# A model of GpSimd's time in a kernel's placement planner, and zero multiplications where the output bank can't take them

## The chip, the cores and the metric

The kernel runs on one core of a Trainium2 chip. The core has five engines that run side by side, each through its own list of instructions in order: TensorE (PE) multiplies matrices into PSUM banks, VectorE (DVE) does elementwise work, ScalarE (ACT) does activations such as exp, GpSimd (POOL) does elementwise work on SBUF data, and SyncE (SP) issues DMAs. They meet through semaphores. The metric is the device time of one execution in microseconds (us); less is better.

## The reference

Two blocks of layers, run twice with the same weights, on x of 2048 rows and 512 columns. Weights and x are bfloat16.

```python
x = x + attention(layernorm(x), wqkv, wo)   # 32 heads of 16, softmax over all 2048 keys
x = x + ffn(layernorm(x), w1, w2)           # 512 -> 1792, silu, 1792 -> 512
x = x + attention(layernorm(x), wqkv, wo)
x = x + ffn(layernorm(x), w1, w2)

def layernorm(x): return (x - mean(x)) / sqrt(var(x) + 1e-5)
def attention(x, wqkv, wo):
    q, k, v = split_heads(x @ wqkv)
    p = softmax(q @ k.T * 16 ** -0.5)       # each of 32 heads: 2048 x 2048
    return join_heads(p @ v) @ wo
```

The 32 x 2048 x 2048 exponentials of each attention are most of the elementwise work.

## The kernel before

**The stream.** Attention of both layers is one stream of 1,024 steps after a first one. A step takes one tile of 128 keys for one group of heads and 512 queries: four heads, so four blocks of 128 x 512 scores. From the twelfth step on, ScalarE takes the exponentials of three blocks (one of 512 columns from its own bank, and a pair of 1,024 columns from one of two double banks; `exp`, L1140), and the fourth block, called d, is done without ScalarE: VectorE turns its scores into the bits of a 16-bit float (`d_y`, in `emit_d`, L1058), and GpSimd adds two constants to those bits for two further terms (`d_z`, in `other_terms`, L1078). In the first twelve steps ScalarE takes four blocks and the fourth shares the bank of d. Scores are multiplications with 32 rows (`score`, L909; tiles `s_ps` and `d_ps`); probabilities times v run every second step into one bank, `o_ps` (`to_o`, L933), which VectorE copies out at the end of a run of steps (`end_run`, L1038: `oA`, `oB`, `oC`, `oT`).

**The background.** Everything else (layer norms, the projections to q, k and v, the output projection, the feed-forward part) is cut into small parts and placed between the steps' instructions. These multiplications all write to one PSUM bank of their own, taken by `bank()`. They are generators that yield a `part(...)`, with what it costs TensorE or VectorE, ahead of each piece.

**The planner.** Engines take no decisions at run time. While the program is built, a `Model` keeps a time for TensorE (`pe`), ScalarE (`act`), VectorE (`dve`) and SyncE (`sp`), and after each step the loop hands out background parts as long as `fits` says that they end before ScalarE needs the next scores. A part may name something that it needs; `Background.done` holds the model's time at which that is ready. If a step gets no work for TensorE, `fill(3)` adds three groups of multiplications with a tile of zeros to the open `o_ps` bank, which leave its sums as they are. It adds none (returns 0) while no run is open in that bank or one of its four parts is still empty or already complete.

**Layer norms.** `ln_stats` (L386) has VectorE take mean and variance of two row tiles (L392, L394), and GpSimd make the reciprocal deviation `rstd` of both: an addition (L396), then a power (L397). `ln_chunk` (L433) has VectorE apply them, `xn` (L402), for the four row tiles of a chunk of 512 rows, and SyncE transpose each by DMA (L308). xn has three buffers, so the fourth norm of a chunk waits until the first transpose has landed. The norms of a chunk are placed by the planner, which in the kernel before knows nothing of GpSimd's time.

**The ends.** The stream is preceded by a prologue of some 16 us and followed by a tail of some 41 us (the last feed-forward chunk), in which instructions are written in a fixed order.

Of the kernel before, what the change touches and what calls it, by code (L numbers as in the profile page):

```python
# [24 lines left out]
def part(dve=0.0, pe=0.0, held=False, sums=False, need=None):  # L25

    return Part(held, pe, dve, sums, need)

class Background:
# [44 lines left out]
    def advance(self, item):  # L74
        if self.model:
            self.model.charge(item[2])
        try:
# [4 lines left out]
            else:  # L82
                home = [q for q in (self.outs, self.side, self.queue) if item in q][0]
                home.remove(item)
                self.done[item[0]] = self.model.landed if self.model else 0.0

    def heads(self, now):
        return [
            self.outs[0] if self.outs else None,
            self.head(now),  # L90
            self.prime(self.side[0]) if self.side else None,
        ]
# [17 lines left out]
class Model:  # L110
# [11 lines left out]
    TRANSPOSE = 1.27  # L122
    TRANSPOSED = 1.7
    DMA = 0.64

    def __init__(self, slack, margin):
        self.slack, self.margin = slack, margin
        self.pe = self.act = self.dve = self.ready = self.free = 0.0
        self.s1 = self.sd = self.copied = self.sp = self.landed = 0.0
        self.s2 = [0.0, 0.0]  # L130
        self.mode = None
        self.early = False
        self.evacuated = 0.0
# [37 lines left out]
    def pv(self, groups):  # L171
        self.pe = max(self.pe, self.copied)
        self.to("V")
        self.pe += self.GROUP * groups
        self.summed = self.pe + self.TO_DVE

    def transpose(self):
        self.sp = max(self.sp, self.dve + 0.1) + self.TRANSPOSE
# [40 lines left out]
def kernel(  # L219
# [39 lines left out]
    FILL = 3  # L259
# [85 lines left out]
    bg = Background()  # L345
# [40 lines left out]
    def ln_stats(c, tiles):  # L386
        n = len(tiles)
        mv = small.tile([P, n, 2], FP32, name="mv", tag="mv", bufs=5)
        for k, i in enumerate(tiles):
            yield part(0.69)  # L390
            st = small.tile([P, 6], FP32, name="st", tag="st")
            nc.vector.bn_stats(st[:], x_sb[c][:, i, :])  # L392
            yield part(0.2)
            nc.vector.bn_aggr(mv[:, k, :], st[:])  # L394
        rstd = small.tile([P, n, 1], FP32, name="rstd", tag="rstd", bufs=5)
        nc.gpsimd.tensor_scalar_add(rstd[:], mv[:, :, 1:2], float(EPS))  # L396
        nc.gpsimd.tensor_tensor(out=rstd[:], in0=rstd[:], in1=half[:, 0:n, :], op=ALU.pow)  # L397
        return mv, rstd
# [20 lines left out]
    def ln_pair(c, i):  # L419

        stats[c, i] = yield from ln_stats(c, (i, i + 1))

    def ln_transpose(i, xns, dst, copy=nc.vector.tensor_copy):

# [8 lines left out]
    def ln_chunk(c, dst):  # L433

        for i in (0, 2):
            mv, rstd = stats.pop((c, i))
            for u in range(2):
                yield part(0.45, need=("xn", xn_count[0] - XN_BUFS))
                xn = ln_apply(c, i + u, mv[:, u, :], rstd[:, u, :])
                transpose(dst[:, i + u, :, :], xn[:])  # L440
                bg.done["xn", xn_count[0]] = bg.model.landed
                xn_count[0] += 1
# [104 lines left out]
    def d_blocks(c):  # L547

        return [(kt, kt % 4) for kt in range(4 * c, 4 * c + 4)]

    def scale_v(L, c):

        n = len(d_blocks(c))
        VB[L, c] = vbpool.tile([P, n * 2 * VBW + 16], FP16, name="VB", tag="VB", bufs=7)
        nc.gpsimd.memset(VB[L, c][:, n * 2 * VBW :], 0.0)
        for i, (kt, j) in enumerate(d_blocks(c)):
            va = VA[L, c][:, kt % 4, 0 : 17 * H].rearrange("p (g j e) -> p g j e", j=4, e=34)
            for k, (_, w) in enumerate(TERMS):
                nc.gpsimd.tensor_scalar(
                    out=VB[L, c][:, (2 * i + k) * VBW : (2 * i + k + 1) * VBW].rearrange(  # L560
                        "p (g e) -> p g e", e=34
                    ),
                    in0=va[:, :, j, :],
                    scalar1=w,
                    scalar2=0.0,
                    op0=ALU.mult,
                    op1=ALU.add,
                )
# [168 lines left out]
    def warm(n, ps=None):  # L737

        if ps is None:
            ps = bank("warm")  # L740
        for i in range(n):
            nc.tensor.matmul(ps, lhsT=ident[:], rhs=w_qkv[:, i % CT, 0:D], start=True, stop=True)  # L742
# [114 lines left out]
    for g in range(NG):  # L857
        mine = [r for r in runs if r[3] == g]
        n = 0
# [46 lines left out]
    def score(blk, out):  # L906
        L, qc, pi, g, par, kt, j = blk
        r = slice(32 * j, 32 * j + 32)
        nc.tensor.matmul(  # L909
            out,  # L910
            lhsT=KT[L, kt // 4][r, g, (kt % 4) * P : (kt % 4 + 1) * P],
            rhs=QT[g][r, par, :],
            start=True,
            stop=True,
        )
# [157 lines left out]
    def other_terms(t, pr):  # L1073

        n = len(pr["ds"])
        for k, (off, _) in enumerate(TERMS):
            z = dpool.tile([P, 2, 512], U16, name=f"d_z{k}", tag=f"z{k}")
            nc.gpsimd.tensor_scalar(  # L1078
                out=z[:, 0:n, :].rearrange("p a b -> p (a b)"),
                in0=pr["y"][:, 0:n, :].rearrange("p a b -> p (a b)"),  # L1080
                scalar1=float(off),
                scalar2=1.0,
                op0=ALU.add,
                op1=ALU.mult,
            )
            for i, d in enumerate(pr["ds"]):
                d["rhs"].append((t + 3 + k, k + 1, z[:, i, :].bitcast(FP16)))

# [14 lines left out]
    with tc.manual_schedule(  # L1103
# [62 lines left out]
        for t in range(1, len(steps)):  # L1166
            a_blks, d_blks = steps[t]
            for L, qc, pi, g, par, kt, j in a_blks + d_blks:
                bg.ensure(q_of[L, qc, pi, g, par])
                if qc == 0:  # L1170
                    bg.ensure(("k", L, kt // 4, g))
            L, qc, pi, g, par, kt, j = a_blks[0]
            if t == len(steps) - NKT:
                load_w1_tail()
            if kt == kts_of[L, qc, pi, g, par][0]:
                for Lq, c, gq, n in q_next.get((L, qc, pi, g, par), []):
                    bg.add(("q", Lq, c, gq, n), proj_q(Lq, c, gq), first=True)
            s2 = score_pair()[:]
            n1 = len(a_blks) - 2
            s1 = [  # L1180
                psum["s"].tile([P, 512], FP32, name="s1_ps", tag=tag, bufs=1)[:]
                for tag in ("s1", "sd")[0:n1]
            ]
            for i in range(2):
                score(a_blks[n1 + i], s2[:, i, :])
            for i in range(n1):
                score(a_blks[i], s1[i])
            if n1 == 1:
                for blk in d_blks:
                    emit_d(t, blk)  # L1190
            m.scores(len(a_blks), len(d_blks))
            while after:
                after.pop()()
                m.sums()
            if t in pv_steps:
                m.pv(emit_pv(t, pv_step(t)))
            if t < D_LEAD:
                p = p_pre[:, 3 * t + 1 : 3 * t + 4, :]
                parts = [p[:, 0:n1, :], p[:, n1 : n1 + 2, :]]
            elif n1 == 1:  # L1200
                p = ppool.tile([P, 3, 512], BF16, name="p_sb", tag="p")
                parts = [p[:, 0:1, :], p[:, 1:3, :]]
            else:
                parts = [
                    dpool.tile([P, 2, 512], U16, name="p_z", tag=f"z{k}")[:].bitcast(BF16)
                    for k in range(2)
                ]
            p_tiles[t] = [p[:, i, :] for p in parts for i in range(p.shape[1])]
            for i in range(n1):
                exp(p_tiles[t][i], s1[i])  # L1210
            exp(flat(parts[1]), flat(s2))
            m.exps(len(a_blks))
            if t <= 4:
                bg.ensure(("v", 0, 0, t - 1))
            if t == 5:
                early[0] = m.early = False
            busy = t in pv_steps
            late = L == 0 or qc == 0
            while True:
                for item in bg.heads(t):  # L1220
                    if bg.fits(item) and (late or not item[2].pe or item[2].sums or t not in pv_steps):
                        break
                else:
                    break
                busy = busy or item[2].pe > 0
                bg.advance(item)
            if n1 == 2 and d_blks:
                m.late_d()
                emit_d(t, d_blks[0])
            if not busy and m.fill_fits(FILL):  # L1230
                n = fill(FILL)
                if n:
                    m.pv(n)
        t = len(steps) + 1
        emit_pv(t, pv_step(t))
        after.pop()()
# [36 lines left out]
```

## Time and profile before

| | us |
|---|---|
| median of three runs | 1564.99 (1564.02 to 1565.08) |
| the profiled execution, its own time | 1566.2 |
| its span, first to last instruction | 1564.1 |
| ScalarE busy in it | 1514.3 (97%) |
| TensorE busy | 1467.9 (94%) |
| GpSimd busy | 1113.9 (71%) |
| VectorE busy | 1080.1 (69%) |

The mean TensorE clock in it was 0.991 of the full one. In the profile, a group of instructions stands in one row: line, engine, operation, tiles out and in, shapes and count; then busy us and the mean ns of one; then the idle time of its engine just ahead of it, and which instruction ended most of that. A waits view lists who waited for whom, with the sum, the number and the longest wait in us. A timeline lists instructions in order of time: start, length, engine and line, how many were merged into the row, and the idle time before it with what ended it. Multiplications are pipelined and their ends are modelled, so busy TensorE isn't TensorE at its peak.

### The profile page before, as it was taken

To read this page: it belongs to the slowest core of one execution; us is meant where nothing else is said; L and a number is where in the kernel's file an instruction comes from. 1 tells how busy PE (TensorE), PEld (TensorE's weight loads), DVE (VectorE), ACT (ScalarE), POOL (GpSimd) and SP (SyncE) were. 2 spreads that over 40 slices of the span, in tenths; PEclk is the share of its full clock that TensorE was granted. 3 is DMA by queue.
4 is the path that set the end of the run, shared out by engine and by line. 5 is a ranking of instruction groups with operands and counts; after the bars stand their busy time and mean duration, and the time that the engine had idled before them with its cause. 6 is when DMAs were issued, how large, how long until landed. Compare 5 with 4: busy or idle time off the path is not lost. (4 is left out here: it accounts for less than half of the span.)

```text
span 1564.1 us, 34241 instructions
## 1 busy us (share of the span) xinstructions
PE 1467.9 (94%) x13361; PEld 464.9 (30%) x13361; DVE 1080.1 (69%) x1733; ACT 1514.3 (97%) x2191; POOL 1113.9 (71%) x1172
## 2 busy tenths in 40 slices
PE   7999998899999999899998999998999899999998
PEld 3222332232322322222322333322332232222225
DVE  6877677667776777667776667676667666676645
ACT  6999999999999999999999999999999999999993
POOL 2888776677876778667876778776777677776760
PEclk9999999999999999999999999999999999999999
DMA  4110013101121112201021010121012101120110
GB/s 138 32 28 2 5 35 65 28 19 44 45 45 28 31 25 50 51 17 42 20 49 42 11 35 9 25 58 32 18 46 62 29 19 30 45 48 22 37 47 14
DMA packets 149442, 55.84 MB, mean 36 GB/s; under 512 B 127776, under 2 KB 148768, under 8 KB 149280
## 3 DMA queue, kind: packets, MB, share of 16 engines
q1 hardware_dynamic: 149280, 53.65, 14.1%
q8 instruction: 105, 1.72, 0.5%
q14 instruction: 57, 0.47, 0.1%
HBM read 28.57 MB, written 4.19 MB: 21 GB/s over the span
## 5 line engine op out<-in xcount | busy, mean ns | idle before, releaser
L1140 ACT ACTIVATE p_sb<-s_ps 128x512 bf16<-128x512 f32 x2026 | 1466.6, 1100 | 9.4 <-PE d_ps L909 5.1
L1058 DVE TENSOR_SCALAR d_y<-d_ps 128x512 uint16<-128x512 f32 x1012 | 697.4, 689 | 404.4 <-PE d_ps L909 362.5
L909 PE MATMUL s_ps<-QT,KT 32*128 32x512 bf16 x3084 | 631.0, 383 | 59.1 <-ACT p_sb L1140 44.9
L909 PE MATMUL d_ps<-QT,KT 32*128 32x512 bf16 x1012 | 390.5, 386 | 9.1 <-DVE d_y L1058 6.0
L909 PEld LDWEIGHTS <-KT 32*128 32x128 bf16 x4096 | 187.1, 91 | 647.9 <-issue 595.1
L933 PE MATMUL o_ps<-p_sb,VA 128*32 128x512 bf16 x3039 | 312.3, 389 | 8.2 <-DVE oB L1038 1.1
L933 PE MATMUL o_ps<-d_y,VA 128*32 128x512 f16 x1012 | 153.7, 380 | 0.0
L933 PEld LDWEIGHTS <-VA 128*32 128x32 bf16 x4096 | 86.7, 95 | 160.9 <-issue 123.0
L711 PE MATMUL f_ps<-w_sb,hT 128*128 128x512 bf16 x392 | 104.0, 382 | 0.0
L933 PEld LDWEIGHTS <-VB 128*32 128x32 f16 x2024 | 78.5, 98 | 55.6 <-issue 1.0
L933 PE MATMUL o_ps<-w_qkv,zero 128*32 128x512 bf16 x1344 | 93.8, 385 | 0.0
L649 ACT ACTIVATE t_sb<-h_ps 128x512 f32<-128x512 f32 x98 | 86.0, 878 | 0.0
L652 DVE SCALAR_TENSOR_TENSOR hT<-t_sb,h_ps 128x512 bf16<-128x512 f32 x98 | 67.3, 687 | 22.5 <-ACT t_sb L649 22.3
L603 DVE TENSOR_TENSOR attn<-ot,rec 128x256 bf16<-128x256 bf16 x45 | 49.3, 1095 | 1.5
L1038 DVE CAST oT<-o_ps 128x512 bf16<-128x512 f32 x64 | 43.6, 681 | 7.7 <-PE o_ps L933 7.7
L402 DVE TENSOR_SCALAR xn<-x,mv,rstd 128x512 bf16<-128x512 bf16 x64 | 42.0, 669 | 4.9 <-DMA fT<-xn 2.7
L392 DVE BATCH_NORM_STATS2 st<-x 128x6 f32<-128x512 bf16 x64 | 43.6, 680 | 2.1 <-DMA x<-in_A_x_dram 2.1
L711 PEld LDWEIGHTS <-hT 128*128 128x128 bf16 x392 | 29.2, 97 | 46.4 <-issue 25.0
L933 PEld LDWEIGHTS <-zero 128*32 128x32 bf16 x1344 | 25.6, 95 | 40.6 <-issue 28.5
L466 PE MATMUL q_ps<-xnT,w_qkv 128*128 128x512 bf16 x136 | 36.6, 389 | 0.0
L466 PE MATMUL k_ps<-xnT,w_qkv 128*128 128x512 bf16 x128 | 35.4, 390 | 0.9 <-DVE xnT L431 0.9
L396 POOL TENSOR_SCALAR rstd<-mv 128x2 f32<-128x2 f32 x32 | 7.7, 239 | 40.0 <-DVE mv L394 38.5
(2298 smaller groups left out, 2093.6 us busy)
## 6 DMA issues: line engine op xcount, KB each, us to landing
wo<-in_A_wo_dram SPq DMA_DIRECT2D x8, 512.0 KB, 3.8
QT<-q SPq DMA_DIRECT2D x240, 16.0 KB, 1.8
x<-in_A_x_dram SPq DMA_DIRECT2D x7, 512.0 KB, 4.2
out_dram<-x SPq DMA_DIRECT2D x16, 128.0 KB, 1.7
w_sb<-in_B_w_dram SPq DMA_DIRECT2D x1, 1792.0 KB, 13.9
w_qkv<-in_A_wqkv_dram SPq DMA_DIRECT2D x3, 512.0 KB, 7.4
w_tail<-in_B_w_dram SPq DMA_DIRECT2D x3, 512.0 KB, 6.9
ot<-oT SPq DMA_TRANSPOSE x45, 2.3
```

Source lines behind the costliest of these rows:

```text
L392: nc.vector.bn_stats(st[:], x_sb[c][:, i, :])
L402: nc.vector.tensor_scalar(out=xn[:], in0=x_sb[c][:, i, :], scalar1=mv[:, 0:1], scalar2=rstd, op0=ALU.subtract, op1=ALU.mult,)
L466: nc.tensor.matmul(ps.rearrange("p (t q) -> p t q", q=P) if len(r.shape) == 3 else ps, lhsT=lhs(ct), rhs=r, start=(ct == 0), stop=(ct == C ...
L603: nc.vector.tensor_tensor(out=attn[L, qc][:, :, P * g : P * (g + 1)].rearrange("p t (j s) -> p t j s", s=32)[:, :, :, 16 * par : 16 * par ...
L649: nc.scalar.activation(t_sb, h_ps, ACT.Tanh, scale=0.5)
L652: nc.vector.scalar_tensor_tensor(out=hT[:, ft, :], in0=t_sb, scalar=1.0, in1=h_ps, op0=ALU.add, op1=ALU.mult)
L711: nc.tensor.matmul(y_ps, lhsT=hT[:, ft, tq * P : (tq + 1) * P], rhs=w2_sb[:, ft, :], start=(ft == 0), stop=(ft == FT - 1),)
L909: nc.tensor.matmul(out, lhsT=KT[L, kt // 4][r, g, (kt % 4) * P : (kt % 4 + 1) * P], rhs=QT[g][r, par, :], start=True, stop=True,)
L933: nc.tensor.matmul(o_tiles[key][32 * j : 32 * j + 32, :], lhsT=lhsT, rhs=rhs, start=(o_count[key][j] == 0), stop=stop,)
L1038: nc.vector.tensor_copy(out=o, in_=o_tiles[key][:])
L1058: nc.vector.tensor_scalar(out=pr["y"][:, len(pr["ds"]), :], in0=s_ps[:], scalar1=float(1024 * SCALE * math.log2(math.e)), scalar2=float(10 ...
L1140: nc.scalar.activation(p_sb, s_ps, ACT.Exp, bias=-SHIFT * math.log(2.0) + math.log(EXP_SUM), scale=float(SCALE),)
```

## The change

Four edits, all in the planner and the loop that places work; no instruction of the computation itself is altered.

1. The model gets a time for GpSimd, `pool`. `pool_busy(us)` lets it begin when VectorE's modelled work is done and returns when it ends. It is charged in three places: by the terms of d (0.65 or 1.1 us), by the scaling of v (2.6 us), and by each pair of statistics (1.0 us).
2. For a pair of statistics the returned time is kept as `done["rstd", c, i]`, and `ln_chunk` yields a part that needs it ahead of the two norms that use it.
3. The call that charges the model for a step's scores stands ahead of the issue of d's instructions instead of behind it.
4. Where `fill` returns 0, the step is past the fifth, the background's bank is free by the model and no background part is under way (`idle`), three full-width multiplications of an identity with columns of the weights are written to the background's bank. Nothing reads them.

```diff
+    def idle(self):
+        return self.active is None and not any(i[2] is not None and i[2].held for i in self.queue)
...
+    ADD = {1: 0.65, 2: 1.1}
...
+    def pool_busy(self, us):
+        self.pool = max(self.pool, self.dve + 0.1) + us
+        return self.pool + 0.1
...
     def ln_pair(c, i):
 
         stats[c, i] = yield from ln_stats(c, (i, i + 1))
+        bg.done["rstd", c, i] = bg.model.pool_busy(1.0) if bg.model else 0.0
...
         for i in (0, 2):
             mv, rstd = stats.pop((c, i))
+            yield part(need=("rstd", c, i))
             for u in range(2):
                 yield part(0.45, need=("xn", xn_count[0] - XN_BUFS))
...
         n = len(d_blocks(c))
+        if bg.model:
+            bg.model.pool_busy(2.6)
...
+            bg.model.pool_busy(bg.model.ADD[n])
             for i, d in enumerate(pr["ds"]):
                 d["rhs"].append((t + 3 + k, k + 1, z[:, i, :].bitcast(FP16)))
...
+            m.scores(len(a_blks), len(d_blks))
             if n1 == 1:
                 for blk in d_blks:
                     emit_d(t, blk)
-            m.scores(len(a_blks), len(d_blks))
...
                 n = fill(FILL)
                 if n:
                     m.pv(n)
+                elif t > 5 and m.free <= m.pe and bg.idle():
+                    warm(FILL)
+                    m.to("B")
+                    m.pe += m.GROUP * FILL
```

`warm` is there in the kernel before, where it is used ahead of and in the tail:

```python
def warm(n, ps=None):
    if ps is None:
        ps = bank("warm")
    for i in range(n):
        nc.tensor.matmul(ps, lhsT=ident[:], rhs=w_qkv[:, i % CT, 0:D], start=True, stop=True)
```

More of the change, by code (lines that the diff above doesn't have):

```diff
@@ L128, in __init__ @@
         self.pe = self.act = self.dve = self.ready = self.free = 0.0
-        self.s1 = self.sd = self.copied = self.sp = self.landed = 0.0
+        self.s1 = self.sd = self.copied = self.sp = self.landed = self.pool = 0.0
         self.s2 = [0.0, 0.0]
```

## The prediction

> **What bounds the kernel now.** I read the page first: the shares of the engines, then the costliest groups.
>
> ```profile
> PE 1467.9 (94%) x13361; PEld 464.9 (30%) x13361; DVE 1080.1 (69%) x1733; ACT 1514.3 (97%) x2191; POOL 1113.9 (71%) x1172
> ...
> L1140 ACT ACTIVATE p_sb<-s_ps 128x512 bf16<-128x512 f32 x2026 | 1466.6, 1100 | 9.4 <-PE d_ps L909 5.1
> ```
>
> ScalarE works for 1514.3 of 1564.1 us, nearly all of it on the exponentials of L1140. So the time is ScalarE's work plus the idle time ahead of it, and an edit that leaves ScalarE's list alone can only win idle time. How much there is in the stream (everything between the first 16 and the last 41 us), the waits of ScalarE say; the columns are the sum in us, the number of waits and the longest.
>
> ```profile
> ACT p_sb L1140 <- PE d_ps L909: 5.1, 9, 1.5
> ACT p_sb L1140 <- PE s_ps L909: 4.2, 4, 2.0
> ACT p_z L1140 <- PE s_ps L909: 2.0, 5, 0.7
> ```
>
> That is 11.3 us, 0.7% of the span: the most that any change of placement in the stream can give. ScalarE also has a small cushion: the same 512-column exponential is recorded at 0.60 us when ScalarE has just been idle and at 0.95 us when work is queued, so up to 0.35 us of lateness shows no idle time at all and costs nothing.
>
> The change speaks of norms that are issued before their rstd exists, so next the tile view of xn, its part on what the engine sat idle for (us, times).
>
> ```profile
>   DMA fT<-xn: 2.7, 1
>   POOL rstd L397: 1.9, 4
> ```
>
> Taken one by one, the records of L402 in the stream that stand behind rstd are those at 33.95 (0.61 us idle), 82.61, 245.88 and 814.38 us (0.07 to 0.08 each); the rest of the 1.9 lies in the prologue and the tail. So only the first is a wait worth the name. VectorE, then ScalarE, in order of time around it:
>
> ```profile
> 32.64 0.70 DVE L402 TENSOR_SCALAR xn<-x,mv,rstd 128x512 bf16<-128x512 bf16 x2
> 33.95 0.41 DVE L402 TENSOR_SCALAR xn<-x,mv,rstd 128x512 bf16<-128x512 bf16 x1 [0.61 <-POOL rstd L397]
> 34.28 0.68 DVE L1058 TENSOR_SCALAR d_y<-d_ps 128x512 uint16<-128x512 f32 x1
> 34.88 0.68 DVE L1038 CAST oA<-o_ps 128x512 bf16<-128x512 f32 x1
> 36.90 0.69 DVE L1058 TENSOR_SCALAR d_y<-d_ps 128x512 uint16<-128x512 f32 x1 [1.34 <-PE s_ps L909]
> ...
> 34.38 0.60 ACT L1140 ACTIVATE p_z<-s_ps 128x512 bf16<-128x512 f32 x1 [0.53 <-PE s_ps L909]
> 35.63 1.51 ACT L1140 ACTIVATE p_z<-s_ps 128x512 bf16<-128x512 f32 x2 [0.66 <-PE s_ps L909]
> ```
>
> Here d_y stands behind the waiting norm, its bank is freed at 34.96, the next scores of that bank start at 35.02 and the exponential of them at 35.63: this wait is ScalarE's.
>
> Last, the TensorE clock. The records show it at half speed in five stretches, 32.1 to 45.7, 86.7 to 90.1, 165.2 to 168.6, 254.0 to 257.4 and 1052.7 to 1056.1 us, all with ScalarE idle in or just before them. Windows, and TensorE's own timeline, at the third (columns of the windows: length, then busy us and instructions of PE, then its clock):
>
> ```profile
> 161.80:165.21 3.41, 2.72 (x28) 1.00 0.00 0
> 165.21:168.63 3.42, 3.42 (x32) 0.50 0.02 5
> ...
> 163.27 0.39 PE L909 MATMUL d_ps<-QT,KT 32*128 32x512 bf16 x1
> 164.19 0.86 PE L909 MATMUL s_ps<-QT,KT 32*128 32x512 bf16 x3 [0.53 <-ACT p_sb L1140]
> ```
>
> [...] (each short stretch lasts 3.41 us, and all edges lie on one 3.41 us grid) [...] xn takes 0.40 us alone and 1.24 us where a d_z of GpSimd runs beside it.
>
> **The change part by part.** A scheduler in the kernel decides the order of its instructions, so what the diff does is read from the two built programs, engine by engine. ScalarE, GpSimd and SyncE have the same lists, instruction for instruction, DMAs included. Moving the call of m.scores and keeping GpSimd's time move nothing else. What differs is this.
>
> *Three norms go later*, all of them the third of their chunk. At step 10 it goes behind one d_y and one oA; at steps 156 and 542 behind one d_y. They are the ones at 33.95, 245.88 and 814.38; the one at 82.61 stays. No bank, transpose or queue order changes.
>
> First norm: the d_ps that its d_y needs is recorded as ending at 33.82. Without the norm d_y can start at 33.86 and end, with its 0.69, at 34.55 instead of 34.96: 0.41 us earlier. The exponential at 35.63 follows to 35.22, its predecessor (34.38 plus a spacing of 0.49) not being in the way, and the rest of this stretch is a chain of single banks (scores, d_y, scores), so it moves too. Gain 0.41. What is late next: the norm itself, now about 35.15, beside GpSimd's d_z, so up to 1.24 us, ending by 36.39; the next d_y is due at 36.90 less 0.41, 36.49, so it still fits, by 0.1. Its transpose, third on SyncE, goes from 35.76 to about 36.4 and the fourth waits for the fourth norm (37.9 before, 37.5 now), so the chunk isn't later; its first reader, k_ps at 43.92, had 1.5 us in hand over the landing at 42.44.
>
> Norm at 245.88: d_y moves up by about 1 us, but at 248.87 the fourth norm waits 2.74 us for the first transpose of its chunk, which sits in SyncE's list behind eight QT copies, an x load and two w1 loads. That landing (251.51) isn't touched, the number of d_y ahead of the fourth norm is the same, and the 2.03 us of ScalarE's idle time at 254.25 count from it. Gain 0. Norm at 814.38: d_y moves up by 1.2 us, what it saves ScalarE is an idle gap of 0.04 at 817.80, the rest was in the cushion. Gain 0.04.
>
> *39 multiplications are added*, three full-width ones of 512 columns at each of 13 steps (91, 95, 99, 103; 611, 647, 655, 663, 767, 883, 899, 995, 1011), between d_ps and the next scores. In the trace TensorE stands idle there for 0.53 us (0.41 at step 103) until an exponential gives its bank back. Consecutive full-width multiplications start 0.216 us apart (q_ps records), the first 0.32 after d_ps (d_ps to q_ps at 995.5), and scores follow the last by 0.31 (k_ps to s_ps at 81.2): 0.32 + 2 x 0.216 + 0.31 = 1.06 us from d_ps, where the trace has 0.91. So the pair of scores is 0.15 late, as it is in any step with three groups; the single score behind it, which ScalarE waits for, comes 1.40 after d_ps, held by its own bank. Cost 0, with 0.3 in hand and the cushion behind that. If all of it were paid, it would be 13 x 0.15 = 2 us, the upper end. The bank they write: its last reader ended 0.73 us or more before d_ps in all 13 places, and its next user comes 2 us or more later. SyncE and VectorE have nothing behind it.
>
> What they give: one of the five half-clock stretches, at 165.2, follows the hole of step 99. With it filled, the window has 0.5 us more work and should keep its clock. ScalarE's idle time inside the stretch is 0.24 at 167.18 and 0.29 at 168.98: gain 0.52. The price of the unknown, from both sides: 0 if the window is still too thin, or if the grid lies elsewhere in the executions that are timed; 1.0 if those executions have two such stretches among the 13 places. I take 0.52. The other four stretches follow holes that get no filling.
>
> Sum: 0.41 + 0 + 0.04 + 0.52 = 0.97 us. The profiled execution took 1566.2 us (span 1564.1, 2.1 around it), so its counterpart should take about 1565.2, span 1563.1. The median of the runs, 1564.99, is 1.2 below the profiled one; 0.97 off it gives 1564.0.
>
> **The rivals.** *The starting stretch runs warm* (faster). If the earlier d_y raises TensorE's activity so that the 13.6 us at half clock from 32.1 end windows earlier, the idle time from 34.38 to 44.06 goes with it: 0.53 + 0.66 + 0.28 + 0.24 + 0.46 + 0.90 = 3.07, so with the other terms up to 3.6 us, 1561.4. For it: every stall there has half-rate scores in its chain. Against: the clock fell before the norm, and the chain of single banks would be thin at full clock too. 4%.
>
> *The multiplications delay the scores* (slower). Place: the single score after each filling. It decides where a filling takes over 1.4 us instead of 0.65 to 1.06, [...]; past the cushion each place would cost up to 0.4, 13 x 0.4 - 0.45 = 4.8, so 1569.7. Against: the background's own k_ps pairs stand in the same place between d_ps and scores and don't cost that. 3%.
>
> *The grid decides* (no change). Norm gain 0.4 alone, or thin places caught elsewhere: from a loss of 0.8 to a gain of 1.6, 1563.4 to 1565.8. 33%. *The sum as worked out*, 1563.4 to 1564.6: 60%.
>
> **How the numbers follow.** About 0.2%, 3.1 us, is what a measurement of this kernel can tell from no change. Likeliest and grid case both lie inside: 93% same, 4% faster, 3% slower. Together they reach from 1563.4 to 1565.8; I stretch the lower end to 1562.6, for half of the first rival or a second stretch saved.
>
> **What would show it.** The idle time before xn at 34 us gone, d_y ahead of it; p_z's wait of 0.66 at 35.6 down to about 0.25; ScalarE's idle time before the exponentials from 11.3 to about 10.4; 39 more warm rows, TensorE's idle time before s_ps behind p_sb down from 44.9 by up to 6.7; no half clock at 165; the 2.7 us behind the transpose still there. I am wrong if ScalarE idles right after a filling, if xn at 35 us delays the next d_y, or if half-clock stretches come in other number than four.

## The result, and the profile after

| | before | changed |
|---|---|---|
| median, runs taken side by side | 1564.51 us (1563.7 to 1567.3) | 1567.31 us (1564.68 to 1568.11) |
| ratio, changed over before | | 1.0013, 95% interval [1.0, 1.0026] |
| profiled execution, own time | 1566.2 us | 1566.83 us |
| its span, and mean TensorE clock | 1564.1 us, 0.991 | 1564.8 us, 0.989 |

The forecast was 1564.0 us with a range of 1562.6 to 1565.9, so this median lies above the range. Six executions are a thin sample: over the study the changed kernel was executed 33 times, with a mean of 1566.14 us (standard error 0.27), and the kernel before 230 times, with a mean of 1565.40 (0.13). The change costs about 0.7 us (standard error 0.3), 0.05%, where 1 us of gain was forecast. No single comparison tells that from no change. Behind it, though, stand gains and losses of up to 3 us, and the experiments could separate the largest.

The page of the changed kernel, engine shares and costliest groups (columns as before):

```profile
PE 1478.7 (94%) x13400; PEld 468.3 (30%) x13400; DVE 1079.5 (69%) x1733; ACT 1514.2 (97%) x2191; POOL 1117.1 (71%) x1172
...
L1153 ACT ACTIVATE p_sb<-s_ps 128x512 bf16<-128x512 f32 x2026 | 1466.4, 1099 | 9.4 <-PE d_ps L921 7.9
```

39 multiplications more on TensorE (of an identity with weights, not of zeros as the title has it), and ScalarE works as long as before. Its idle time ahead of the exponentials is 9.4 us again, but the part put down to d_ps went from 5.1 to 7.9. The waits of ScalarE (sum, number, longest):

```profile
ACT p_sb L1153 <- PE d_ps L921: 7.9, 11, 3.5
...
ACT p_sb L1153 <- PE s_ps L921: 1.4, 4, 0.5
ACT p_z L1153 <- PE s_ps L921: 1.2, 5, 0.3
```

The sum fell from 11.3 to 10.5, close to the 10.4 that was forecast, but not by the steps that were forecast. The 4.2 behind s_ps held the wait of 2.0 at step 156. That wait is now 3.5 us long and is put down to d_ps; without it the two rows went from 2.2 to 1.4 and from 5.1 to 4.4. The tile view of xn shows where VectorE waited:

```profile
  DMA fT<-xn: 4.1, 2
  POOL rstd L405: 1.2, 2
```

rstd gave back 0.7 us; the transpose of xn takes 1.4 us more. The start of the stream, VectorE and then ScalarE, in order of time:

```profile
32.45 0.70 DVE L410 TENSOR_SCALAR xn<-x,mv,rstd 128x512 bf16<-128x512 bf16 x2
33.37 0.69 DVE L1070 TENSOR_SCALAR d_y<-d_ps 128x512 uint16<-128x512 f32 x1 [0.22 <-PE s_ps L921]
33.98 0.68 DVE L1050 CAST oA<-o_ps 128x512 bf16<-128x512 f32 x1
34.58 0.84 DVE L410 TENSOR_SCALAR xn<-x,mv,rstd 128x512 bf16<-128x512 bf16 x1
36.00 0.69 DVE L1070 TENSOR_SCALAR d_y<-d_ps 128x512 uint16<-128x512 f32 x1 [0.58 <-PE s_ps L921]
...
33.90 0.60 ACT L1153 ACTIVATE p_z<-s_ps 128x512 bf16<-128x512 f32 x1 [0.28 <-PE s_ps L921]
34.73 1.51 ACT L1153 ACTIVATE p_z<-s_ps 128x512 bf16<-128x512 f32 x2 [0.23 <-PE s_ps L921]
```

d_y stands ahead of the norm, the norm doesn't wait and isn't in the next d_y's way, and the exponentials that stood at 34.38 and 35.63 start at 33.90 and 34.73 (0.19 us of this is a shorter prologue in this execution). The windows around the first fillings (columns: length, then busy us and instructions of PE, PEld, DVE, ACT and POOL, then the TensorE clock):

```profile
160.00:163.40 3.40, 3.40 (x38) 1.05 (x36) 1.43 (x3) 3.40 (x6) 2.68 (x3) 1.00 0.00 0
163.40:166.80 3.40, 3.34 (x37) 0.99 (x36) 2.56 (x4) 3.40 (x7) 2.60 (x4) 1.00 0.02 5
```

TensorE is full where a window had 2.72 us of work, ScalarE does not idle, and the half clock at 165 is gone. So the two intended effects are there. The largest loss is at step 156. VectorE and ScalarE there, of the kernel before:

```profile
251.61 0.41 DVE L402 TENSOR_SCALAR xn<-x,mv,rstd 128x512 bf16<-128x512 bf16 x1 [2.74 <-DMA fT<-xn]
...
254.25 1.51 ACT L1140 ACTIVATE p_sb<-s_ps 128x512 bf16<-128x512 f32 x2 [2.03 <-PE s_ps L909]
256.75 2.95 ACT L1140 ACTIVATE p_sb<-s_ps 128x512 bf16<-128x512 f32 x4 [0.99 <-PE d_ps L909]
```

and of the changed kernel:

```profile
245.35 0.69 DVE L1070 TENSOR_SCALAR d_y<-d_ps 128x512 uint16<-128x512 f32 x1
245.96 0.57 DVE L410 TENSOR_SCALAR xn<-x,mv,rstd 128x512 bf16<-128x512 bf16 x1
246.62 0.69 DVE L1070 TENSOR_SCALAR d_y<-d_ps 128x512 uint16<-128x512 f32 x1
251.08 0.41 DVE L410 TENSOR_SCALAR xn<-x,mv,rstd 128x512 bf16<-128x512 bf16 x1 [3.77 <-DMA fT<-xn]
...
254.73 1.51 ACT L1153 ACTIVATE p_sb<-s_ps 128x512 bf16<-128x512 f32 x2 [3.47 <-PE d_ps L921]
257.10 2.99 ACT L1153 ACTIVATE p_sb<-s_ps 128x512 bf16<-128x512 f32 x4 [0.85 <-PE d_ps L921]
```

The fourth norm waits 3.77 us for the landing of the first transpose, where it waited 2.74; the d_y behind it on VectorE starts at 251.41, TensorE idles for 2.78 us ahead of the d_ps at 252.14 (2.30 in the kernel before), and ScalarE idles for 3.47 us where it idled for 2.03. The clock is at half for two windows from 251.0, where it was for one from 254.0.

The stream's lengths, from end to end of ScalarE's pairs of blocks, summed by stretches of steps, give the whole account of the two profiled executions. Of those not listed, the prologue differs by 0.19 us and no other by more than 0.07.

| us | before | after | |
|---|---|---|---|
| steps 9 to 30 | 35.19 | 34.91 | first norm |
| 90 to 110 | 28.87 | 28.13 | half clock gone |
| 150 to 175 | 41.45 | 42.84 | norm of step 156 |
| 540 to 600 | 91.40 | 91.26 | norm of step 542 |
| 695 to 715 | 33.85 | 32.21 | ScalarE idle for 1.52 at 1054.35, now 0.17; cause open |
| 800 to 880 | 119.67 | 120.21 | half clock at 1206.7 |
| tail | 40.91 | 42.56 | half clock at 1534.4 |
| prologue and the rest | 1172.77 | 1172.65 | |

### The profile page after: what moved, and what is told of

It reads as the page before. It is cut to its first block, busy times and chain, and to the rows that moved or that the text cites. A ratio compares the mean times of both kernels' runs of the same rounds, so it can differ in the third digit from the quotient of the medians.

```text
span 1564.8 us, 34320 instructions
## 1 busy us (share of the span) xinstructions
PE 1478.7 (94%) x13400; PEld 468.3 (30%) x13400; DVE 1079.5 (69%) x1733; ACT 1514.2 (97%) x2191; POOL 1117.1 (71%) x1172
## 5 line engine op out<-in xcount | busy, mean ns | idle before, releaser
L476 PE MATMUL k_ps<-xnT,w_qkv 128*128 128x512 bf16 x128 | 35.4, 389 | 1.4 <-DVE xnT L440 0.9
```

Source lines behind the costliest of these rows:

```text
L476: nc.tensor.matmul(ps.rearrange("p (t q) -> p t q", q=P) if len(r.shape) == 3 else ps, lhsT=lhs(ct), rhs=r, start=(ct == 0), stop=(ct == C ...
```

## The experiments

In the expectations, theory A says that the clock's grid alone decides (the half-clock stretches of one trace begin and end on a grid of 3.41 us, which runs through 32.09 us in before and through 32.52 in after), B that the work of the fillings costs time, C that the moved norms do. Theory D came up after the first runs. The trace has two DMA queues whose kind is instruction. The one that matters here (q8) moved 105 packets of 16 KB, 0.9 to 1.7 us each; the other (q14) moved smaller packets, of up to 8 KB. The packets of q8 keep step with TensorE: from the start of one to the start of the next, TensorE begins a median of 256 instructions in the trace of before (205 to 296) and 256.5 in that of after (212 to 294). So I take them for the fetches of TensorE's list; the trace doesn't name an owner. A packet of q8 is called a fetch from here on. D says that a longer list of TensorE moves these fetches to earlier places in the stream, where they hold up the DMA transposes. Theory E is C for the norm of step 156 alone. Where the text says longer list, 24 or more instructions were added to TensorE's list ahead of step 150 and none taken away.

Executions of one kernel spread over up to 10 us, and a median of a dozen moves by 1 us and more when it is taken again. So each line below has the ratio with its interval and the mean of its executions with the standard error; stage lengths are from the one profiled execution.

**The change again.** The same kernel, twice more (labels a_again and changed_3).

> The changed kernel once more, unaltered. Theory A (the grid decides): the stream itself is about 1 us shorter than before, and the time of an execution is a base plus a cost for each 3.41 us window in which TensorE's clock is halved; [...] single executions of the changed kernel and of the kernel before both spread over some 1563.5 to 1568 us, and the ratio of the two is anywhere from 0.9995 to 1.002. Theory B (the fillings cost): every execution is 2 to 3 us over the kernel before, whatever the number of half-clock windows. Theory C (the moved norms cost): the same as B here. What tells A from B and C in this run is the relation of time to mean clock over its executions: by A executions with the same mean clock as the kernel before take about 1 us less, by B and C they take 2 us more.

> The changed kernel a third time, for its mean on this chip. Both theories: 1566 to 1567, ratio 1.0005 to 1.0013, as its 19 executions so far.

Measured: 1.0007 [0.9998, 1.0016], mean 1565.99 (0.47) of 13; and 1.0 [0.999, 1.001], mean 1565.95 (0.39) of 14. The first median was high. Steps 150 to 175 took 42.09 and 42.95, the tail 42.55 and 42.56.

**Each part alone.** norms_only leaves out the fillings, and was run twice; fills_only leaves the norms where they were.

```diff
# norms_only
-                elif t > 5 and m.free <= m.pe and bg.idle():
-                    warm(FILL)
-                    m.to("B")
-                    m.pe += m.GROUP * FILL
# fills_only
-            yield part(need=("rstd", c, i))
```

> The changed kernel without the fillings: the three norms are moved, TensorE's list is that of the kernel before. Theory A: stream 0.4 to 0.7 us shorter than before, ratio 0.9990 to 1.001, spread by half-clock windows. Theory B (the fillings cost): 1564 to 1564.5, ratio 0.9995. Theory C (the moved norms cost): about 1567, ratio 1.0015, with the stall behind the fourth norm of step 158 longer than before in its profile.

> The changed kernel without the wait for rstd: 39 multiplications at 13 steps are added, VectorE's list is that of the kernel before. Theory A: ScalarE not idle behind any filling, no half clock in the 13 places, time as before or up to 0.5 us less, ratio 0.9990 to 1.001. Theory B: about 1567, ratio 1.0015, with idle time of ScalarE or a half clock that begins right behind fillings. Theory C: 1564.5, ratio 1.000.

> The moved norms alone, a second time. Theory D: nothing of the loss is theirs, ratio 0.9995 to 1.0003. Theory C: 1.0005 or more again.

Measured: norms alone 1.0007 [0.9999, 1.0015] and 1.0007 [0.9996, 1.0019], over both 1566.57 (0.36), 1.2 above before. Fillings alone 1.0008 [0.9998, 1.0018], 1566.90 (0.61), 1.5 above. Neither half gains. norms_only has steps 150 to 175 at 42.29 and 41.59. fills_only has something else. Waits of TensorE for k_ps in fills_only (sum, number, longest):

```profile
PE k_ps L475 <- DMA xnT<-xn: 2.4, 2, 1.7
```

The 1.7 us is at step 618. A wait that long there is in no trace of a kernel with before's list of TensorE. ScalarE idles behind it, and steps 600 to 695 take 136.04 instead of 133.63. There a fetch begins at 930.33, 1.35 us long, among the packets of the fourth transpose of xn, which lands 10.95 us after the end of step 611 instead of 9.11. With before's list the same fetch begins 1.2 steps later, behind the landing. The changed kernel has the list of fills_only there. In two traces of it (changed_3, and tail_filled, which differs only in the tail) the fetch begins at 9.13 and 8.59 after the end of step 611, the landing is at 11.13 and 10.98, and steps 600 to 695 take 136.32 and 136.28. In the two others (after and a_again) it begins at 10.34 and 10.18 and nothing is late. So the place of a fetch also varies from execution to execution. That led to theory D.

**The tail.** 10 instead of 6 multiplications of an identity with columns of weights, in the pause of TensorE ahead of the tail's last transposes, in the changed kernel, in before, and in two others below. (The expectation of list_back_tail further down has 40, 24 and zeros; the edit is this one.)

```diff
-        warm(6)
+        warm(10)
```

> The changed kernel with ten multiplications instead of six in the tail's pause ahead of the last transposes, so that TensorE has work until the normalised tiles are there (the four more are read by nothing). In the one profiled execution the clock was halved in the tail, which took 1.65 us more than before. Theory A: no half clock in the tail in any execution; the slow executions of 1567 to 1568 us lose some 1.6 us, so the median is 1564 to 1566. Theories B and C: the tail isn't the cause, the median stays near 1567.

> The kernel before with ten multiplications instead of six in the tail's pause. If a half clock in the tail costs 1.65 us and falls on about one execution in three, as two of six profiles so far have it, the mean is about 0.5 us under the kernel before (1564.5 against 1565.1) and no execution has a tail over 41.2 us. If the tail isn't caught in the kernel before, there is no difference.

> The same, and ten instead of six multiplications in the tail's pause. Theory D with the half clock in the tail: another 0.3 to 0.6 us less, 1563.5 to 1564.5, ratio 0.9985 to 0.9995, faster than both kernels. Theory A (nothing but the grid): 1565 to 1566 in the mean.

Measured: 1.0006 [0.9998, 1.0014], mean 1565.62 (0.38); on before 0.9995 [0.9986, 1.0004], 1564.90 (0.35); on the kernel with a realigned list (changed_aligned, below) 0.9999 [0.9991, 1.0008], 1565.28 (0.39), against 1565.82 (0.32) without. The tail took 40.9 us in all four profiles that have these multiplications, and 42.55 or 42.56, with a half-clock window, in four of the sixteen others. One in four at 1.65 gives an estimated 0.4 us on average; the means are in line with that, but every interval includes 1.0, so no gain is shown.

**What comparing a kernel with itself gives.**

> The kernel before, unaltered, in the place of a changed kernel: what a comparison of this kernel with itself shows. Theory A (the grid decides, and some 13 executions don't average it out): ratio between 0.999 and 1.001, and as much as 1.0007 would not be strange, so the ratios of 1.0006 to 1.0008 seen so far say nothing. Theory D (the fillings make TensorE's instruction list longer, so its fetches by DMA, 16 KB and about 1.3 us each, fall elsewhere, and one of them now hits a transpose that TensorE waits for): ratio 1.000, clearly under that of the kernels with fillings, and in its profile the fetch near step 618 begins at 618 and the transposes ahead of it land 2.4 us after their issue.

Measured: 1.0001 [0.9992, 1.001], mean 1565.71 (0.37), 0.3 above the mean of all executions of before. In this execution the half clock at 165 wasn't there without any filling (28.13 for steps 90 to 110).

**The length of the list alone.** before with a prologue of 71 multiplications of 100 columns instead of 56 of 128, so the same work in 30 more instructions (a weight load each); and the reverse, 41 of 176.

```diff
# list_shifted
-            for i in range(56):
-                nc.tensor.matmul(w_ps[:, 0:P], lhsT=ident[:], rhs=ident[:], start=True, stop=True)
+            for i in range(71):
+                nc.tensor.matmul(w_ps[:, 0:100], lhsT=ident[:], rhs=ident[:, 0:100], start=True, stop=True)
# list_back, in place of the same two lines
+            wide = const.tile([P, 176], BF16, name="wide")
+            nc.vector.memset(wide[:], 0.0)
+            for i in range(41):
+                nc.tensor.matmul(w_ps[:, 0:176], lhsT=ident[:], rhs=wide[:], start=True, stop=True)
```

> The kernel before with no filling and no moved norm, but with 71 warming multiplications of 100 columns in the prologue instead of 56 of 128: about the same work, and 30 instructions more ahead of everything else in TensorE's list, as many as the fillings have put there by step 611. Theory D: as slow as the fillings alone, some 1 to 2 us over the kernel before (1566 to 1567), the fetch of step 618 begins at 617, and in some executions the fourth transpose of step 616 lands 1.8 us late. Theory A: 1563.5 to 1566 as the kernel before, ratio 1.000 within 0.001.

> The kernel before with 30 instructions more ahead of TensorE's list, a second time: its 14 executions averaged 1567.8, 2.5 us over the kernel before. Theory D: again 1.5 to 3 us over the kernel before, ratio 1.001 to 1.002. Theory A: back to a ratio of 1.000 within 0.0007.

> The kernel before with 41 warming multiplications of 176 columns instead of 56 of 128: nothing but 30 instructions fewer ahead of TensorE's list. Theory D: not the same time as the kernel before, by up to 2 us either way, since the fetches come about one step later than before; waits on DMA landings stand at other steps. Theory A: the mean within 0.6 of the kernel before, the same steps waiting on DMA.

Measured: 30 more, 1.0009 [0.9998, 1.002] and 1.0028 [1.0019, 1.0037], over both 1568.51 (0.44): 3.1 us slower. 30 fewer, 0.9994 [0.9987, 1.0001], 1564.42 (0.39). Instructions that do nothing for the stream and don't lengthen the prologue (it ends at 15.98 and 16.09, before's at 15.98 to 16.19) make the kernel slower by 0.2%. The place that D had named was missed: the fetch began at step 619, and the transpose of step 616 landed on time, at 9.12 and 9.11. Other places were hit. At step 997 a fetch begins 8.51 and 8.61 us after the end of step 990, and the transpose of ot (the attention output, transposed by DMA) lands at 11.15 in both traces instead of 8.89. VectorE waits 1.06 us for it, and steps 1000 to 1024 take 34.69 and 35.64 instead of 33.76.

Step 149 has such a pair in every trace, and there the two groups part cleanly. Times are from the end of step 150, and ot is issued at -4.66 in each. In the eight traces with a longer list a fetch begins at -3.70 to -3.50, and ot lands at -0.78 to 0.12. In the twelve others the fetch begins at -1.85 or later, and ot lands at -2.31 to -1.35. In the two list_shifted traces, with every norm in its place, steps 150 to 175 take 41.94 and 42.28. So that the list's length acts on the time is shown by experiment, and that it acts through fetches beside transposes fits every trace. How a fetch holds up a transpose was not shown: the trace doesn't name the DMA engine of a packet.

**Fillings with the list shifted back.** fills_only, and the changed kernel, each with 30 fewer instructions in the prologue.

```diff
# fills_shifted_back, on fills_only
-            for i in range(56):
+            for i in range(41):
# changed_aligned: the four lines of list_back, on the changed kernel
```

> The fillings alone, with 41 warming multiplications in the prologue instead of 56, so that from step 103 to 611 TensorE's list stands within 6 instructions of where it stood before. Theory D: no late transpose at step 616, 1 to 2 us less than the fillings alone, so 1564 to 1565.5. Theory A: spread as the others, 1564 to 1567. Theory B (a filling costs by itself): 1566 to 1567, as the fillings alone.

> The changed kernel whole, with 41 warming multiplications of 176 columns in the prologue instead of 56 of 128: the same work there, but 30 instructions fewer, so from step 611 on TensorE's list stands within 48 instructions behind of where it stood in the kernel before. Theory D (the longer list moves the fetches onto transposes): no late transpose at step 616, the mean 1 to 2 us under the 1566.3 of the changed kernel, so 1564 to 1565, ratio 0.999 to 1.000. Theory B (a filling costs by itself) and theory C (the moved norms cost): 1566 to 1567.

> The changed kernel with 30 instructions fewer ahead of TensorE's list, a second time, beside the changed kernel on one chip. Theory D: 0.7 to 1.5 us under the changed kernel of this call, ratio to the kernel before 0.9993 to 1.000. Theories B and C: as the changed kernel.

Measured: fills_shifted_back 1.0003 [0.9995, 1.0012], 1566.27 (0.38); in its trace, with the shorter prologue, the clock fell at 10 us, and the stream started 1.64 us later than with 56 multiplications. So 1.64 us of its profiled time belong to the prologue and not to the fillings. The wait of k_ps at step 618 is gone (133.63), and steps 150 to 175 took 39.66. changed_aligned 0.9998 [0.999, 1.0007] and 1.0001 [0.9991, 1.0012], over both 1565.82 (0.32): no clear gain on the changed kernel, and steps 150 to 175 stayed at 42.07 and 42.25. So the list wasn't all of it.

**Fillings of no size.** The three multiplications cut to 8 columns: the same instructions, hardly any work.

```diff
-                    warm(FILL)
+                    ps = bank("warm")
+                    for i in range(FILL):
+                        nc.tensor.matmul(ps[:, 0:8], lhsT=ident[:], rhs=w_qkv[:, i, 0:8], start=True, stop=True)
```

> The changed kernel with its 39 added multiplications cut from 512 columns to 8 each: TensorE's list is as long and in the same places, the work in the 13 holes is almost nothing. Theory D (list length): no better than the changed kernel, 1566 to 1568, ratio 1.0005 to 1.002, and the half clock at step 94 to 98 may come back. Theory B (the work of the fillings costs): as the kernel before or better, 1564.5 to 1565.3, ratio 0.9995 to 1.000.

Measured: 1.0005 [0.9996, 1.0015], 1566.76 (0.32), not better than the full ones, so B's forecast failed. By itself this isn't conclusive, as the profile has ten half-clock stretches where after has six, which may hide a gain. But in the trace of after ScalarE isn't idle in the 4 us behind any of the 13 fillings. The half clock of steps 90 to 110 is back (28.86, at 164.0 us). Of the ten traces with full fillings none has it there, of the ten without them (or with these small ones) four do, which speaks for the work of the fillings as what removes it.

**One norm back in its place.** On changed_aligned, the wait for rstd is left out for the chunk of step 156 alone. One xn goes back ahead of its d_y on VectorE; every other list, TensorE's with it, is the same.

```diff
-    def ln_chunk(c, dst):
+    def ln_chunk(c, dst, wait=True):
...
-            yield part(need=("rstd", c, i))
+            if wait: yield part(need=("rstd", c, i))
...
-        yield from ln_chunk(c, fTs[L, c])
+        yield from ln_chunk(c, fTs[L, c], wait=(L, c) != (0, 0))
```

> The changed kernel with its prologue of 41 wide multiplications (so its list of TensorE is 30 instructions shorter from the start), and the third norm of step 156 alone put back ahead of its d_y; nothing else differs on any engine. Theory E, the move of this norm costs: ScalarE's stage from step 150 to 175 goes from some 42.1 us (as with the norm moved) to between 38.6 and 41.0, and the mean of the times lies about 1.2 us below the same kernel with the norm moved (1565.8 over its two runs), so near 1564.6; ratio 0.9992 to 0.9998. Theory A, the grid alone decides: the stage stays between 41 and 43 and the mean near 1565.8.

Measured: 0.9979 [0.9971, 0.9986], median 1561.83, mean 1561.87 (0.34) of 20. That is 4.0 us below the same kernel with the norm moved and 3.5 below before, and steps 150 to 175 took 38.81 instead of 42.07. Theory E holds, and its price was put too low. VectorE and ScalarE of changed_norm156_back:

```profile
243.37 1.71 DVE L410 TENSOR_SCALAR xn<-x,mv,rstd 128x512 bf16<-128x512 bf16 x2
245.00 0.67 DVE L1070 TENSOR_SCALAR d_y<-d_ps 128x512 uint16<-128x512 f32 x1
246.13 0.69 DVE L1070 TENSOR_SCALAR d_y<-d_ps 128x512 uint16<-128x512 f32 x1 [0.46 <-PE d_ps L921]
247.82 0.41 DVE L410 TENSOR_SCALAR xn<-x,mv,rstd 128x512 bf16<-128x512 bf16 x1 [0.99 <-DMA fT<-xn]
...
250.41 4.32 ACT L1155 ACTIVATE p_sb<-s_ps 128x512 bf16<-128x512 f32 x6 [0.24 <-PE d_ps L921]
```

and of changed_aligned:

```profile
244.05 0.69 DVE L1070 TENSOR_SCALAR d_y<-d_ps 128x512 uint16<-128x512 f32 x1 [0.22 <-PE d_ps L921]
244.66 0.48 DVE L410 TENSOR_SCALAR xn<-x,mv,rstd 128x512 bf16<-128x512 bf16 x1
245.46 0.69 DVE L1070 TENSOR_SCALAR d_y<-d_ps 128x512 uint16<-128x512 f32 x1 [0.31 <-PE d_ps L921]
249.28 0.41 DVE L410 TENSOR_SCALAR xn<-x,mv,rstd 128x512 bf16<-128x512 bf16 x1 [3.13 <-DMA fT<-xn]
...
252.94 1.51 ACT L1155 ACTIVATE p_sb<-s_ps 128x512 bf16<-128x512 f32 x2 [2.84 <-PE d_ps L921]
255.31 1.51 ACT L1155 ACTIVATE p_sb<-s_ps 128x512 bf16<-128x512 f32 x2 [0.85 <-PE d_ps L921]
```

With the norm moved, counted from the end of step 150, the two d_y stand 1.02 and 0.75 us earlier, but the fourth norm begins 1.39 later. The first transpose was issued at the same time in both, 8.05 and 8.06 us after the end of step 150. What differs ahead of the landing is TensorE's fetch. From the packets, in us from the end of step 150:

```
kernel                 d_y of steps 156, 157   fetch            first transpose   steps 150-175
                                                                issued  landed
changed_norm156_back     9.04   10.17          11.49 to 12.63    8.05   11.76       38.81
list_back                9.04   10.17          11.96 to 13.35    8.04   11.73       38.62
before_tail              9.04   10.17          11.76 to 12.92    8.05   11.99       40.54
before                   9.03   10.17          11.49 to 12.58    8.18   13.50       41.45
before_again             9.03   10.17          11.27 to 12.51    8.19   13.50       40.86
norms_only               8.02    9.42          11.34 to 12.44    8.05   13.34       42.29
changed_aligned          8.02    9.42          11.06 to 12.21    8.06   13.15       42.07
changed_aligned_2        8.02    9.42          10.86 to 12.05    8.15   13.34       42.25
```

The other five traces in which it is issued at 8.04 to 8.26 agree: landed at 11.74 and 12.01 with the fetch at 12.00 and 11.80 (list_back_tail, fills_shifted_back), at 13.25 to 13.51 with the fetch at 10.35 to 11.28 (changed_aligned_tail, tail_filled, norms_only_2).

The d_y went up, and the next fetch begins 0.43 us or more earlier in the three realigned kernels with the norm moved (10.67 to 11.06) than in changed_norm156_back. That TensorE, running ahead, brings the fetch forward is my inference from this order. In changed_norm156_back the first transpose was all but through when the fetch came, and the second took the hit: it landed at 13.80, 2.0 behind the first. In changed_aligned the packets of the transposes ended at 270 to 290 per 0.25 us up to 11.5, and from 11.75 to 13.0 at 1 to 10 per 0.25 us; one that ended after 13.0 had taken 1.5 us. An early landing isn't all of it: in before_tail and fills_shifted_back the fourth norm begins at 12.09 and 12.10, 0.02 and 0.03 behind a d_z of GpSimd, and takes 1.17 and 1.16 us, and ScalarE then idles for 1.23; in changed_norm156_back it begins at 11.86, ahead of the d_z at 12.07, takes 0.41, and ScalarE idles for 0.24. The windows around the waits say the rest. Of changed_norm156_back, the stretch that holds its wait:

```profile
247.00:250.40 3.40, 2.85 (x37) 0.72 (x34) 1.71 (x3) 3.13 (x5) 2.38 (x3) 1.00 0.85 125
```

Of changed_aligned, the last window of its wait and the one behind it:

```profile
249.57:252.98 3.41, 2.64 (x18) 0.53 (x18) 1.42 (x4) 0.57 (x2) 1.17 (x2) 0.50 0.17 38
252.98:256.39 3.41, 3.41 (x20) 0.71 (x18) 1.99 (x3) 2.56 (x4) 1.20 (x2) 0.50 0.00 0
```

The columns end with clock, DMA share and GB/s. In changed_aligned the clock falls behind the longer hole (the window from 246.16, with 2.04 us of work, comes just before), and the work behind the landing starts at half speed, for two windows. The stretch loses 3.26 us in all.

**Both small gains on before.** The prologue of list_back and the tail of before_tail.

> The kernel before with the prologue of 41 wide multiplications (30 instructions of TensorE fewer from the start) and 40 instead of 24 multiplications of zeros ahead of the tail's first. If the two gains seen singly (ratios 0.9994 and 0.9995, both with intervals that reach 1.0) are real and add up: ratio 0.9985 to 0.9993, mean near 1564.0, half clock in the tail absent. If they were scatter: ratio 0.9996 to 1.0004.

Measured: 0.9994 [0.9983, 1.0004], 1564.68 (0.45). They don't add up; list_back alone had 1564.42.

## Why the prediction was wrong

- *First norm, gain 0.41*: right in its mechanism, and in the profile of after 0.28 over steps 9 to 30. Over all profiles, those with the norm moved have a mean of 34.6 there and those without 35.4, so with the clock's part (see the rival below) it was nearer 0.8; with the half clock at four windows, seven profiles with the norm moved have 34.9, so the term by itself was an estimated 0.5.
- *Norm at 245.88, gain 0*: **the step that failed.** The premise "That landing (251.51) isn't touched" was false. I looked at SyncE's list, which is the same, and so at the time of issue, which is the same too. In the runs the landing went with the fetch beside it as well: at 11.76 with one that began at 11.49 (changed_norm156_back), at 13.15 with one at 11.06 (changed_aligned). In place of 0 the runs showed 3.3 us by the stage and 4.0 (0.5) by the means, on the realigned list. On before's list it is less, about 1 us by the stage (42.29 and 41.59 against 41.45, 40.86 and 40.54), since before's fetch lies at the edge and its landing is mostly late already (13.50 and 13.50, 11.99 once). The second part of the step, that d_y going up changes nothing behind the landing, was wrong as well: the hole ahead of it grew, and in the realigned kernels the clock fell behind it for two windows.
- *Norm at 814.38, gain 0.04*: 0.14 in every trace.
- *39 multiplications, cost 0*: right for the places themselves. In the trace of after no ScalarE idle time follows a filling, and the slow rival, that they delay the scores, didn't come. Wrong as to their number: "ScalarE, GpSimd and SyncE have the same lists, instruction for instruction, DMAs included" left out the 105 packets of 16 KB. 24 of the 78 added instructions stand ahead of step 150 and 30 are in by step 611, and the fetches moved (the one near step 149 begins at -3.69 us from the end of step 150 in after, at -1.74 in before); 30 instructions with nothing else cost 3.1 (0.5) us.
- *What they give, 0.52*: 0.74 against before, which had the half clock there, and none in the executions without a half clock there, as in before_again.
- *The rival that the start runs warm* didn't come in the profile of after, where the half clock of four windows is there, from 32.5. It came in a small part elsewhere: in four of the eleven profiles with the norm moved it lasts three windows, and steps 9 to 30 take 34.05 to 34.28. One profile without the moved norm has three windows too, at 35.15. The rival that the grid decides was right about single stretches (90 to 110: 28.87 in before, 28.13 in before_again; the tail: 40.9 or 42.55), but steps 150 to 175 take 41.59 to 42.29 in all five profiles of kernels with the norm moved and no longer list, and 38.62 to 41.45 in the seven with the norm in its place, so it doesn't decide the largest term.
- *"The other four stretches"*: after had six, with one in the tail worth 1.65 us.
- *The end of the stream* came 1.00 us earlier than before, which meets the 0.97 of the sum by luck: it contains +1.39 for step 156, +0.54 for a half clock, and -1.64 at step 702, none of which was forecast.
- *The range* took three executions within 0.07% for the spread of the kernel. 230 executions of before have a standard deviation of 1.9 us and reach from 1561.84 to 1572.00. They sort by mean clock: 1563.4 at 0.993, 1565.2 at 0.991, 1567.5 at 0.988, so time goes with the clock at an estimated 0.9 us for each half-clock window of 3.41 us (0.0011 of the mean); not all of it need be the clock's doing: beside the window at 254.0 in before, ScalarE idles for 2.03 us, up to 254.25. Of the 3.3 us between the forecast and the median of six, about 1.2 is scatter of those six, since all 33 executions have a mean of 1566.14.

Open: in the changed kernel as it is, with its longer list, the norm of step 156 wasn't put back by itself. fills_only, where all norms are in their place on that list, took 43.77 there, so more than the norm is needed: with the longer list a transpose of ot lands late at step 149, as shown above, and SyncE begins the QT copies at 2.1 instead of 1.0. changed_norm156_back itself is one run of 20 executions. The net 0.7 (0.3) us of the change can't be shared out among its parts more exactly than that.

## What to carry to other kernels

Before a DMA landing is called untouched, look at what else moves data at that time, the instruction fetches of a long unrolled list included: here one norm moved behind its d_y went with a fetch 0.43 us earlier, and 30 more instructions with 3.1 us more time. A thing that is moved "for free" ahead of a stall that hangs on a transfer can make the stall longer: here from 0.99 to 3.13 us, with two windows at half clock behind it. Put a gain back together from its parts by experiment: here the change without one of its three moves, and with its list 30 instructions shorter, is faster than before by 0.21% [0.14, 0.29], while the whole is not.

## What was not expected of the hardware

- The length of TensorE's list acts on the time (3.1 us for 30 instructions): with a fetch of 16 KB, 0.9 to 1.7 us long, among its packets, a transpose of xn landed at 10.95 instead of 9.11 us after a fixed event (the end of step 611), and at 13.15 instead of 11.76 (step 150).
- A sharp edge: a fetch that began at 11.49 hit the first transpose in one kernel, issued 0.13 us later, and just missed it in another (13.50 against 11.76).
- The recorded busy time of a window doesn't say whether half clock follows. On the grid of the trace of before, the window at 161.80 with 2.72 us was followed by it, and those at 151.56 with 2.72, 168.63 with 2.74 and 267.61 with 2.20 weren't; in changed_tiny one with 2.89 (160.56) was. The ends of multiplications are modelled, and what the clock goes by stays open. That the filled window of step 99 would keep its clock was my estimate.
